# Infini-attention and gated MLP on one core: two head groups share a round of logits, and memory read and update move ahead of the product with V, into its banks

## The chip, the core and the metric

One core of a Trainium2 chip runs the whole program. The metric is device time in microseconds (us). TensorE, VectorE, ScalarE and GpSimd are called PE, DVE, ACT and POOL in the profile; the kernel writes a list of instructions of its own for each (the page of before counts 5369 on PE, 769 on DVE, 347 on ACT and 241 on POOL), and makes them wait for each other through semaphores. All executions quoted are within 1.5% of the fastest of the same kernel; each also reports the mean clock that TensorE was granted, as a share of full speed.

## The reference, cut to what matters

```python
def _A_ref(x, wq, wk, wv, wo, beta):          # H = 32 heads of 32, N = 4 segments of L = 512 tokens
    ...
    for s in range(N):
        qs, ks, vs = ...                      # of this segment
        p = _softmax(einsum('bhqd,bhkd->bhqk', qs, ks) * scale + mask)
        a_dot = einsum('bhqk,bhkd->bhqd', p, vs)
        pq = phi(qs)                          # phi(t) = t + 1 where t > 0, else exp(t)
        num = einsum('bhld,bhde->bhle', pq, M)
        den = einsum('bhld,bhd->bhl', pq, z)[..., None] + 1e-06
        o = g * (num / den) + (1.0 - g) * a_dot
        pk = phi(ks)
        M = M + einsum('bhld,bhle->bhde', pk, vs)
        z = z + einsum('bhld->bhd', pk)
    return o @ wo
h = x + _A_ref(_layernorm(x), ...)            # then h + a gated MLP of _layernorm(h), unchanged here
```

Causal attention inside a segment, plus a read of a memory (M, z) that all earlier segments wrote, mixed by a gate.

## The kernel before

Heads go in groups of four, eight groups a segment, so 32 runs n = 8 s + c of one loop body. Four heads' logits share a round: four matmuls with 32 contraction rows each, one per quarter of the array's rows, into banks 0 to 3; one exponential then evicts all four banks. Because the mask is causal, key chunk j (128 keys) needs 512 - 128 j query columns: rounds of chunk 0 (512 columns), chunks 1 and 3 (384 + 128) and chunk 2 (256). In the unused right half of the third round's banks the memory read is placed.

```python
    def logits(n, rnd):
        parts = {0: ((0, 0, 512),), 1: ((1, 0, 384), (3, 384, 128)), 2: ((2, 0, 256),)}[rnd]
        ...
        for j, o, w in parts:
            for i in range(4):
                pe.matmul(PS[:, i, o:o + w], qk[32 * i:32 * (i + 1), 1, j * 128:(j + 1) * 128],
                          qk[32 * i:32 * (i + 1), 0, j * 128:512], ..., tile_position=(32 * i, 0))
        if rnd == 2 and n >= NQ:
            mem(n)                                   # 4 matmuls into PS[:, cq, 256:388]
        act.activation(e[:, :, 0:wid], PS[:, 0:4, 0:wid], ACTF.Exp, scale=float(SCALE))
        ...                                          # POOL masks the diagonal blocks
        if rnd == 2 and n >= NQ:
            mem_norm(n)                              # DVE: + eps, reciprocal, one 512-wide multiplication

    # a run n (segments 1 and 2)
        logits(n, 0)
        fill(f1)                  # key projection of group n + 1
        pv(n - 1)                 # product with V of the last group: 40 matmuls into banks 4 and 5, then norm on DVE
        logits(n, 1)
        state(n - 1)              # memory update: 4 matmuls into a rotating bank, 2 DVE operations
        bg_pop()                  # a step of a layer norm (DVE)
        fill(f2)                  # query projection of group n + 1
        logits(n, 2)
        phi_exp(n + 1)            # ACT
        fill(f3)                  # half of a V or output projection
        phi_max(n + 1); bg_pop()
        fill(f4); bg_pop()        # the other half
```

Projections use the only two rotating banks, 6 and 7. A recording layer adds a semaphore wait for every hazard; for PSUM it works by whole banks, so that an engine never touches a bank while another one may. That is a choice of the code.

The softmax here doesn't subtract the row's maximum and nothing guards it: scores larger than these inputs give would overflow.

Of the kernel before, what the change touches and what calls it, by code (L numbers as in the profile page):

```python
# [5 lines left out]
BF16 = mybir.dt.bfloat16  # L6
F32 = mybir.dt.float32
I32 = mybir.dt.int32
ACTF = mybir.ActivationFunctionType
# [248 lines left out]
def bass_sequential_preLN__memory_aug_infini_attn__mixer_gmlp__prompt_kernel(  # L258
# [86 lines left out]
    PQK = [b2("pqk%d" % i, [128, 2, L], BF16) for i in range(2)]  # L345
    ETMP = b2("etmp", [128, 2, L], BF16)
    PK = [b2("pk%d" % i, [128, 4, 128], BF16) for i in range(3)]
    E = [[b2("e%d%d" % (k, i), [128, 4, w], BF16) for i, w in enumerate((512, 512, 256))] for k in range(2)]
    TA = b2("ta", [128, 4, 4, 32], F32)
    TM = [b2("tm%d" % i, [128, 4, 4, 32], F32) for i in range(2)]  # L350
    V = b2("v", [128, 4, H, 34], BF16)
# [20 lines left out]
    def bank(b):  # L372
        return PS[:, b, :]

    PVX = PS[:, 4:6, :].rearrange("p b (h w) -> p (b h) w", w=256)
    PVA = PVX[:, :, 0:132].rearrange("p q (i w) -> p q i w", w=33)

    rot = {"banks": list(range(8)), "n": 0}

    def next_bank():  # L380
        b = rot["banks"][rot["n"] % len(rot["banks"])]
        rot["n"] += 1
        return b
# [89 lines left out]
                dve.tensor_copy(d, v)  # L473


    def v_out(s, tcl, half, b):
        o = V[:, tcl, 16 * half:16 * half + 16, 0:32]
        v = bank(b).rearrange("p (h d) -> p h d", d=32)
        if (s, tcl, half) == (0, 3, 0):
            dve.tensor_single_scalar(o, v, RS0[tcl][:], ALU.mult)  # L480
        else:
            act.activation(o, v, ACTF.Copy, scale=RS0[tcl][:] if s == 0 else 1.0)

# [1 line left out]
        pe.matmul(bank(b), XNT[s % 2][:, i, tcl * 128:(tcl + 1) * 128], WV[half][:, i, :],  # L485
                  start=(i == 0), stop=(i == 7))

    def proj_v(s, tcl, half):
        b = next_bank()
        for i in range(8):  # L490
            v_mm(s, tcl, half, b, i)
        v_out(s, tcl, half, b)

    def proj_qk(n, which):
        s, c = divmod(n, NQ)
        b = next_bank()
        xt = XNT[s % 2]
        w = WK if which else WQ
        mm8(bank(b), lambda i: w[:, i, c * 128:(c + 1) * 128], lambda i: xt[:, i, :])
        qk_out(n, which, b)  # L500

    def qk_out(n, which, b):
        if n < NQ:
            dve.tensor_tensor(QK[n % 2][:, which, :], bank(b), RB[:], ALU.mult)
        else:
            act.activation(QK[n % 2][:, which, :], bank(b), ACTF.Copy)

# [16 lines left out]
            sp.dma_start_transpose(PK[n % 3][:], PQK[n % 2][:, 1, :])  # L524


    def logits(n, rnd):
        qk = QK[n % 2]
        parts = {0: ((0, 0, 512),), 1: ((1, 0, 384), (3, 384, 128)), 2: ((2, 0, 256),)}[rnd]
        wid = (512, 512, 256)[rnd]  # L530
        e = E[n % 2][rnd]
        for j, o, w in parts:
            for i in range(4):
                pe.matmul(PS[:, i, o:o + w], qk[32 * i:32 * (i + 1), 1, j * 128:(j + 1) * 128],
                          qk[32 * i:32 * (i + 1), 0, j * 128:512], start=True, stop=True,
                          tile_position=(32 * i, 0))
        if rnd == 2 and n >= NQ:
            mem(n)
        act.activation(e[:, :, 0:wid], PS[:, 0:4, 0:wid], ACTF.Exp, scale=float(SCALE))
        for j, o, w in parts:  # L540
            d = e[:, :, o:o + 128]
            pool.affine_select(out=d, in_=d, pattern=[[0, 4], [1, 128]], compare_op=ALU.is_ge, fill=0.0,
                               base=0, channel_multiplier=-1)
        if rnd == 2 and n >= NQ:
            mem_norm(n)

    def pv(n, cqs=range(4)):
        c = n % NQ
        for cq in cqs:
            for j in range(cq + 1):  # L550
                rnd, o = {0: (0, cq * 128), 1: (1, cq * 128 - 128), 2: (2, cq * 128 - 256), 3: (1, 384)}[j]
                for i in range(4):
                    pe.matmul(PVA[:, cq, i, :], E[n % 2][rnd][:, i, o:o + 128], V[:, j, 4 * c + i, 0:33],
                              start=(cq % 2 == 0 and j == 0 and i == 0), stop=False, skip_group_check=True)
        if 3 in cqs:
            norm(n)

    def mem(n):
        c = n % NQ
        for cq in range(4):  # L560
            pe.matmul(PS[:, cq, 256:388], PQK[n % 2][:, 0, cq * 128:(cq + 1) * 128], MZB[:, c, :, 0:33],
                      start=True, stop=True)

    def mem_norm(n):
        om = PS[:, 0:4, 256:388].rearrange("p q (i d) -> p q i d", d=33)
        dve.tensor_single_scalar(RDM[:], om[:, :, :, 32], float(MEM_EPS), ALU.add)
        dve.reciprocal(RDM[:], RDM[:])
        dve.tensor_tensor(TM[n % 2][:], om[:, :, :, 0:32], RDM[:].unsqueeze(3).to_broadcast([128, 4, 4, 32]), ALU.mult)

    def norm(n):  # L570
        s, c = divmod(n, NQ)
# [9 lines left out]
        if c == NQ - 1:  # L581
            for tcl in range(4):
                to_T(OT, tcl, OTOK[s % 2][:, tcl, :])

    def state(n):
        s, c = divmod(n, NQ)
        if s == NSEG - 1:
            return
        b = next_bank()
        for tcl in range(4):  # L590
            pe.matmul(PS[:, b, 0:132], PK[n % 3][:, tcl, :], V[:, tcl, 4 * c:4 * c + 4, 0:33],
                      start=(tcl == 0), stop=(tcl == 3))
        if s == 0:
            dve.tensor_copy(MSUM[:, c, :], PS[:, b, 0:132])
        else:
            dve.tensor_tensor(MSUM[:, c, :], MSUM[:, c, :], PS[:, b, 0:132], ALU.add)
        dve.tensor_tensor(MZB[:, c, :, 0:33], MSUM[:, c, :].rearrange("p (i d) -> p i d", d=33), MASKG[:, c, :, :],
                          ALU.mult)


    def xr_load(tc):
# [80 lines left out]
    for i in range(4, 8):  # L682
        for t in range(2):
            v_mm(0, t, 0, vb[t], i)
    pe_Th(3, c3, act, dve)
    act_var(3)
    rstd0(3)
    var0(ln_stats(XCH[2]))
    rstd0(2)
    diag(0)  # L690
    v_out(0, 0, 0, vb[0])
    diag(1)
    diag(3)
    diag(2)
    v_out(0, 1, 0, vb[1])
    proj_v(0, 2, 0)
    gates()
# [25 lines left out]
    def z2_group(k, tc, stage=None):  # L723
        s, tcl = divmod(tc, 4)
        b = next_bank()
        wi = WIN[k % 3]
        mm8(PS[:, b, 0:448], lambda i: HNT[s][:, i, tcl * 128:(tcl + 1) * 128], lambda i: wi[:, i, 0:448])
        if stage is None:
            z2_gelu(k, tc, PS[:, b, 0:448])
        else:  # L730
            act.activation(ZSTG[stage][:], PS[:, b, 0:448], ACTF.Copy)
            staged.append((k, tc, ZSTG[stage][:]))

    def z2_gelu(k, tc, src):
# [17 lines left out]
    LAST = NSEG * NQ - 1  # L752
    for n in range(LAST + 1):
        s, c = divmod(n, NQ)
        f1, f2, f3, f4 = [], [], [], []
        if n < LAST:
            f1, f2 = [("qk", n + 1, 1)], [("qk", n + 1, 0)]
        if s == 0:
            f3 = [("v", 0, c, 1)] if c < 4 else [("v", 1, c - 4, 0)]
        elif s < NSEG - 1:  # L760
            if c < 2:
                f3, f4 = [("v", s, 2 * c, 1)], [("v", s, 2 * c + 1, 1)]
            elif c < 6:
                f3, f4 = [("wo", s - 1, c - 2, 0)], [("wo", s - 1, c - 2, 1)]
            else:
                f3, f4 = [("v", s + 1, 2 * (c - 6), 0)], [("v", s + 1, 2 * (c - 6) + 1, 0)]
        elif c < 2:
            f3, f4 = [("v", s, 2 * c, 1)], [("v", s, 2 * c + 1, 1)]
        elif c < 6:
            f3, f4 = [("wo", s - 1, c - 2, 0)], [("wo", s - 1, c - 2, 1)]  # L770
        elif c == 6:
            f3, f4 = [("z2", 0, 4, 0)], [("z2", 0, 5, 1)]
        else:
            f1, f2 = [("z2", 0, 6, 2)], [("z2", 0, 7, 3)]
            f3, f4 = [("z2", 0, 0)], [("z2", 0, 1)]

        def fill(lst):
            for u in lst:
                {"v": proj_v, "wo": wo, "qk": proj_qk, "z2": z2_group}[u[0]](*u[1:])

        if s < NSEG - 1 and c < 4:
            ln_tasks(XCH[c], XNT[(s + 1) % 2], c)
        if s < NSEG - 2 and c >= 4:
            x_load(4 * (s + 2) + c - 4)
        if s > 0 and c == 1:
            xr_load(4 * (s - 1))

        if n == 0:
            fill(f1)
            f1 = [("v", 0, 3, 0)]  # L790
        logits(n, 0)
        fill(f1)
        if n > 0:
            pv(n - 1, range(3) if s == NSEG - 1 else range(4))
        logits(n, 1)
        if s == NSEG - 1:
            pv(n - 1, (3,))
        if n > 0:
            state(n - 1)
        bg_pop()  # L800
        fill(f2)
        logits(n, 2)
        if n < LAST:
            phi_exp(n + 1)
        while n == LAST and staged:
            z2_gelu(*staged.pop(0))
        fill(f3)
        if n < LAST:
            phi_max(n + 1)
        bg_pop()  # L810
        fill(f4)
        bg_pop()
        if n == 1:
            sp.dma_start(WO[:], wcols(A_wo, 0, D))
        if n in (24, 26):
            win_load((n - 24) // 2)
# [101 lines left out]
```

## Time and profile before

| | before |
|---|---|
| time, median (range) | 802.24 us (801.92 to 802.71, 4 runs) |
| granted TensorE clock | 1.000 |
| TensorE busy, by the page | 793.6 us, 99% |
| attention, runs 8 to 31 (first logits to the end of the last product with V, by starts) | 228.1 us |
| two runs of segments 1 and 2 | 19.14 to 19.26 us |

The page's totals and, from its second part, the busy tenths and granted clock in 40 slices:

```profile
PE 793.6 (99%) x5369; PEld 379.8 (47%) x5369; DVE 379.5 (47%) x769; ACT 297.9 (37%) x347; POOL 129.2 (16%) x241
...
PE   8999999999999999999999999999999999999998
...
PEclk9999999999999999999999999999999999999999
```

The ends of matmuls are modelled and overlap (a 512-column matmul of the gated MLP has 379 ns in the page, but 224 of them in a row start 0.216 us apart, 579.04 to 627.39), so 99% busy does not say that nothing is lost. The starts do. This is the timeline of TensorE for one run of segment 2 (start, length, operation, output and inputs, shape, how many; a bracket would be an idle time):

```profile
156.90 0.40 PE L209 MATMUL ps<-qk 32*128 32x512 bf16 x4
157.23 1.90 PE L209 MATMUL ps<-xnT,wk 128*128 128x512 bf16 x8
158.97 1.16 PE L209 MATMUL ps<-v,e 128*128 128x33 bf16 x40
160.05 0.40 PE L209 MATMUL ps<-qk 32*128 32x384 bf16 x8
160.38 0.41 PE L209 MATMUL ps<-v,pk 128*128 128x132 bf16 x4
160.63 1.89 PE L209 MATMUL ps<-xnT,wq 128*128 128x512 bf16 x8
162.45 0.29 PE L209 MATMUL ps<-qk 32*128 32x256 bf16 x4
162.67 0.41 PE L209 MATMUL ps<-mzb,pqk 128*128 128x132 bf16 x4
162.92 3.62 PE L209 MATMUL ps<-wv,xnT 128*128 128x512 bf16 x16
166.47 0.39 PE L209 MATMUL ps<-qk 32*128 32x512 bf16 x4
```

No bracket, no idle time. But the query projection starts at 160.63 and the next round at 162.45: 1.82 us for eight matmuls that owe 8 x 0.216 = 1.73. And that round holds TensorE for 0.22 us (162.45 to 162.67) where its 256 columns owe 0.11 by my estimate (half of the 0.216 for 512 columns, with the four quarters taken as side by side: the four 512-column matmuls of a first round hold TensorE for 0.33 us, 156.90 to 157.23, not for 4 x 0.216). Each round costs about 0.095 us before it and 0.11 after it. That is nearly the whole of what TensorE loses in these runs: from 84 to 310 us, which is all but the start of run 8 and a little after run 31, rounds account for 14.6 of the 15.3 us that starts show beyond the steady spacing of matmuls. Segments 1 to 3 have 72 rounds.

The other engines have their own durations (groups of instructions; busy total, mean ns of one, idle time before them):

```profile
L209 DVE TENSOR_TENSOR tm<-ps,rdm 128x512 f32<-128x512 f32 x24 | 16.6, 692 | 0.8
...
L209 DVE BATCH_NORM_STATS2 stats<-hch 128x6 f32<-128x512 bf16 x32 | 22.1, 690 | 0.6
L209 DVE TENSOR_TENSOR hch<-xr,ps 128x512 bf16<-128x512 bf16 x32 | 21.7, 680 | 5.6 <-PE ps L209 5.1 <-issue 0.5
...
L209 DVE TENSOR_TENSOR msum<-msum,ps 128x132 f32<-128x132 f32 x16 | 4.5, 284 | 0.0
```

And the chain of work that ended last, followed back, is TensorE nearly throughout:

```profile
PE 95%; DVE 4%; ACT 0%; issue 0%
```

### The profile page before, as it was taken

What the parts mean: (1) busy time and instruction counts of PE and PEld (TensorE: products, weight loads), DVE (VectorE), ACT (ScalarE), POOL (GpSimd) and SP (SyncE); (2) the same over time, 40 slices, a digit from 0 to 9 for tenths busy, and PEclk for the clock granted to TensorE, in tenths of its full rate; (3) what the DMA queues carried; (4) which work ended last, traced back from release to release, by engine and by line L of the source; (5) the groups of instructions that cost most, each with busy time, mean ns of one, the idle gap of its engine ahead of it and who ended that gap; (6) DMA issues with size and microseconds to landing.
All of it is one profiled execution on the core that took longest, in us unless ns stands there. A gap on an engine that the chain in (4) does not pass through costs nothing.

```text
span 800.3 us, 12483 instructions
## 1 busy us (share of the span) xinstructions
PE 793.6 (99%) x5369; PEld 379.8 (47%) x5369; DVE 379.5 (47%) x769; ACT 297.9 (37%) x347; POOL 129.2 (16%) x241
## 2 busy tenths in 40 slices
PE   8999999999999999999999999999999999999998
PEld 3444455554454445455544444444444444444444
DVE  6775688579843775844562000053234323323432
ACT  5777877877778675133333333100000000000000
POOL 3543333333333331100131000000000000000000
PEclk9999999999999999999999999999999999999999
DMA  9662535353515324611116000650270143022002
GB/s 295 174 165 53 93 81 120 85 105 84 95 31 127 113 54 112 159 47 53 52 54 132 1 0 1 203 107 7 79 132 1 33 117 69 0 66 47 1 7 86
DMA packets 125000, 64.79 MB, mean 81 GB/s; under 512 B 94992, under 2 KB 113936, under 8 KB 124944
## 3 DMA queue, kind: packets, MB, share of 16 engines
q1 hardware_dynamic: 124944, 63.99, 33.0%
q8 instruction: 42, 0.69, 0.4%
q14 instruction: 14, 0.11, 0.1%
HBM read 32.51 MB, written 8.39 MB: 51 GB/s over the span
## 4 chain that ended last, share of the span: by engine, by line
PE 95%; DVE 4%; ACT 0%; issue 0%
PE ps L209 95%; DVE stats L209 1%; ACT e L209 0%; DVE ta L209 0%; DVE otok L209 0%; DVE hch L209 0%; DVE diag L209 0%; DVE rd L209 0%; DVE xnT L209 0%; DVE pqk L209 0%; DVE lno L209 0%; DVE mv L209 0%; DVE mzb L209 0%; DVE etmp L209 0%; DVE rdm L209 0%
## 5 line engine op out<-in xcount | busy, mean ns | idle before, releaser
L209 PE MATMUL ps<-wspT,z 128*128 128x512 bf16 x896 | 194.0, 379 | 0.0
L209 ACT ACTIVATE e<-ps 128x2048 bf16<-128x2048 f32 (+1 forms) x96 | 152.8, 1592 | 49.3 <-PE ps L209 48.8
L209 PEld LDWEIGHTS ps<-wspT,z 128*128 128x128 bf16 x896 | 87.7, 98 | 105.7
L209 DVE TENSOR_TENSOR tmpg<-ps,brow 128x512 f32<-128x512 f32 x56 | 38.7, 691 | 197.0 <-DMA brow<-in_B_b_sp_dram 105.4
L209 POOL TENSOR_SCALAR_AFFINE_SELECT e<-e 128x512 bf16<-128x512 bf16 x128 | 83.9, 667 | 178.6 <-ACT e L209 178.5
L209 PE MATMUL ps<-win,hnT 128*128 128x448 bf16 x512 | 98.3, 352 | 0.0
L209 PE MATMUL ps<-w_out,yT 128*128 128x512 bf16 (+2 forms) x462 | 97.4, 373 | 0.0
L209 PE MATMUL ps<-hnT,win 128*128 128x512 bf16 x448 | 96.9, 379 | 0.0
L209 PEld LDWEIGHTS ps<-win,hnT 128*128 128x128 bf16 x512 | 49.8, 98 | 46.3 <-issue 0.2
L209 PEld LDWEIGHTS ps<-w_out,yT 128*128 128x128 bf16 x462 | 44.7, 98 | 52.3
L209 PEld LDWEIGHTS ps<-hnT,win 128*128 128x128 bf16 x448 | 43.8, 98 | 52.8
L209 PE MATMUL ps<-xnT,wk 128*128 128x512 bf16 x256 | 60.8, 380 | 0.0
L209 PE MATMUL ps<-xnT,wq 128*128 128x512 bf16 x256 | 60.5, 379 | 0.0
L209 PE MATMUL ps<-wv,xnT 128*128 128x512 bf16 x256 | 59.1, 379 | 0.2 <-ACT xnT L209 0.2
L209 ACT ACTIVATE z<-ps 128x448 bf16<-128x448 f32 x60 | 32.5, 543 | 69.4 <-PE ps L209 69.4
L209 PE MATMUL ps<-wo,oT 128*128 128x512 bf16 x256 | 57.9, 379 | 0.0
L209 ACT ACTIVATE z1T<-ps 128x512 bf16<-128x512 f32 x56 | 33.4, 597 | 63.3 <-PE ps L209 63.3
L209 DVE TENSOR_TENSOR fin<-fin,ps 128x512 bf16<-128x512 bf16 (+2 forms) x33 | 22.1, 671 | 71.3 <-DMA fin<-out_dram 40.8
L209 DVE BATCH_NORM_STATS2 zst<-z 128x6 f32<-128x448 bf16 x64 | 38.9, 620 | 30.1 <-ACT z L209 30.1
L209 PEld LDWEIGHTS ps<-v,e 128*128 128x128 bf16 x1280 | 37.3, 96 | 9.1 <-issue 1.7
L209 DVE TENSOR_TENSOR yT<-tmpg,z1T 128x512 bf16<-128x512 f32 x56 | 38.8, 692 | 1.9
L209 PE MATMUL ps<-v,e 128*128 128x33 bf16 x1280 | 38.4, 177 | 0.0
(83 smaller groups left out, 574.8 us busy)
## 6 DMA issues: line engine op xcount, KB each, us to landing
xch<-in_A_x_dram SPq DMA_DIRECT2D x16, 256.0 KB, 3.0
xr<-in_A_x_dram SPq DMA_DIRECT2D x16, 256.0 KB, 3.2
out_dram<-hch SPq DMA_DIRECT2D x16, 256.0 KB, 2.5
fin<-out_dram SPq DMA_DIRECT2D x16, 256.0 KB, 2.8
out_dram<-fin SPq DMA_DIRECT2D x31, 128.0 KB, 1.7
win<-in_B_w_in_dram SPq DMA_DIRECT2D x4, 896.0 KB, 5.1
w_out<-in_B_w_out_dram SPq DMA_DIRECT2D x1, 3584.0 KB, 13.7
win<-in_B_w_in_dram SPq DMA_DIRECT2D x3, 1024.0 KB, 5.1
```

The lines of the kernel that those rows point to most:

```text
L209: ins = getattr(e, op.name)(*op.args, **op.kw)
```

## The change

The intent: from segment 1 on, the 256-column third rounds of two neighbouring groups fill one 512-column round, so a pair of groups takes five rounds and not six. The memory read can then no longer use the empty half of those banks. It moves, together with the memory update, to a place one run ahead: half of it into bank 5, beside the product with V (which is packed 171 columns apart so that query chunks 0 to 2 stand in bank 4 and chunk 3 in bank 5), the other half into the rotating bank of the update. Some evictions move from ACT to DVE, and the start is reordered a little. The core of the diff (cut: buffers, arguments passed through):

```diff
-    PVX = PS[:, 4:6, :].rearrange("p b (h w) -> p (b h) w", w=256)
-    PVA = PVX[:, :, 0:132].rearrange("p q (i w) -> p q i w", w=33)
+    PSF = PS[:].rearrange("p b n -> p (b n)")
+    PVA = PSF[:, 2048:2048 + 4 * 171].rearrange("p (q w) -> p q w", w=171)[:, :, 0:132]
+    PVA = PVA.rearrange("p q (i w) -> p q i w", w=33)
...
+    def memory(n):
+        s, c = divmod(n, NQ)
+        b = next_bank()
+        if s > 0:
+            mo = [PSF[:, 2700 + 132 * i:2832 + 132 * i] for i in range(2)]        # bank 5
+            mo += [PS[:, b, 132 + 132 * i:264 + 132 * i] for i in range(2)]
+            for cq in range(4):
+                pe.matmul(mo[cq], PQK[n % 2][:, 0, cq * 128:(cq + 1) * 128], MZB[:, c, :, 0:33], ...)
+        if s < NSEG - 1:
+            ...                                             # the update's 4 matmuls into PS[:, b, 0:132]
+        if s > 0:
+            om = [PS[:, b, 132:396], PSF[:, 2700:2964]]
+            ...
+            for k in range(2):                              # + eps; one reciprocal after both
+                dve.tensor_single_scalar(RDM[:, q, :], om[k][:, :, :, 32], float(MEM_EPS), ALU.add)
+            ...
+            for k in range(2):
+                q = slice(2 - 2 * k, 4 - 2 * k)
+                dve.tensor_tensor(TM[n % 2][:, q, :, :], om[k][:, :, :, 0:32], ..., ALU.mult)
+        ...                                                 # msum, mzb on DVE
...
-            f1, f2 = [("qk", n + 1, 1)], [("qk", n + 1, 0)]
+            f1 = [("qk", n + 1, 1, act if first else dve)]  # first: n is even
+            f2 = [("qk", n + 1, 0)]
...
+        if s > 0 and not first:
+            logits([(n - 1, 2), (n, 2)])                    # the shared round
+            fill(f1)
+            memory(n - 1)
+            bg_pop()
+            logits([(n, 0)])
+            fill(f2)
+            pv(n - 1)
+            logits([(n, 1), (n, 3)])
+            if n == LAST:
+                memory(n)
+        elif s > 0:
+            logits([(n, 0)])
+            fill(f1)
+            memory(n - 1)
+            pv(n - 1)
+            bg_pop()
+            logits([(n, 1), (n, 3)])
+            fill(f2)
```

and in the start:

```diff
+    var0(ln_stats(XCH[2]))
+    rstd0(2)
     pe_Th(3, c3, act, dve)
     act_var(3)
     rstd0(3)
-    var0(ln_stats(XCH[2]))
-    rstd0(2)
     ...
+    diag(2)
     diag(3)
-    diag(2)
```

More of the change, by code (lines that the diff above doesn't have):

```diff
@@ L347, in bass_sequential_preLN__memory_aug_infini_attn__mixer_gmlp__prompt_kernel @@
     PK = [b2("pk%d" % i, [128, 4, 128], BF16) for i in range(3)]
-    E = [[b2("e%d%d" % (k, i), [128, 4, w], BF16) for i, w in enumerate((512, 512, 256))] for k in range(2)]
+    E = [[b2("e%d%d" % (k, i), [128, 4, 512], BF16) for i in range(2)] for k in range(2)]
+    E2 = b2("e2", [128, 4, 512], BF16)
     TA = b2("ta", [128, 4, 4, 32], F32)
@@ L473, in pe_T, with v_out @@
                 dve.tensor_copy(d, v)
-    def v_out(s, tcl, half, b):
+    def v_out(s, tcl, half, b, eng=act):
         o = V[:, tcl, 16 * half:16 * half + 16, 0:32]
@@ L480, in v_out @@
             dve.tensor_single_scalar(o, v, RS0[tcl][:], ALU.mult)
+        elif eng is dve:
+            dve.tensor_copy(o, v)
         else:
@@ L486, in v_mm, with proj_v @@
                   start=(i == 0), stop=(i == 7))
-    def proj_v(s, tcl, half):
+    def proj_v(s, tcl, half, eng=act):
         b = next_bank()
@@ L491, in proj_v, with proj_qk @@
             v_mm(s, tcl, half, b, i)
-        v_out(s, tcl, half, b)
-    def proj_qk(n, which):
+        v_out(s, tcl, half, b, eng)
+    def proj_qk(n, which, eng=act):
         s, c = divmod(n, NQ)
@@ L499, in proj_qk, with qk_out @@
         mm8(bank(b), lambda i: w[:, i, c * 128:(c + 1) * 128], lambda i: xt[:, i, :])
-        qk_out(n, which, b)
-    def qk_out(n, which, b):
+        qk_out(n, which, b, eng)
+    def qk_out(n, which, b, eng=act):
         if n < NQ:
             dve.tensor_tensor(QK[n % 2][:, which, :], bank(b), RB[:], ALU.mult)
+        elif eng is dve:
+            dve.tensor_copy(QK[n % 2][:, which, :], bank(b))
         else:
@@ L524, in phi_max, with e_of, logits @@
             sp.dma_start_transpose(PK[n % 3][:], PQK[n % 2][:, 1, :])
-    def logits(n, rnd):
-        qk = QK[n % 2]
-        parts = {0: ((0, 0, 512),), 1: ((1, 0, 384), (3, 384, 128)), 2: ((2, 0, 256),)}[rnd]
-        wid = (512, 512, 256)[rnd]
-        e = E[n % 2][rnd]
-        for j, o, w in parts:
+    def e_of(n, j, cq):
+        o = (cq - j) * 128
+        if j == 2:
+            return E2, 256 * (n % 2) + o
+        return E[n % 2][j % 2], o + (384 if j == 3 else 0)
+    def logits(parts):
+        for n, j in parts:
+            qk = QK[n % 2]
+            e, o = e_of(n, j, j)
+            w = 512 - 128 * j
             for i in range(4):
@@ L536, in logits @@
                           tile_position=(32 * i, 0))
-        if rnd == 2 and n >= NQ:
-            mem(n)
-        act.activation(e[:, :, 0:wid], PS[:, 0:4, 0:wid], ACTF.Exp, scale=float(SCALE))
-        for j, o, w in parts:
+        lo = e_of(*parts[0], parts[0][1])[1]
+        hi = o + w
+        act.activation(e[:, :, lo:hi], PS[:, 0:4, lo:hi], ACTF.Exp, scale=float(SCALE))
+        for n, j in parts:
+            o = e_of(n, j, j)[1]
             d = e[:, :, o:o + 128]
@@ L543, in logits @@
                                base=0, channel_multiplier=-1)
-        if rnd == 2 and n >= NQ:
-            mem_norm(n)
     def pv(n, cqs=range(4)):
@@ L550, in pv @@
             for j in range(cq + 1):
-                rnd, o = {0: (0, cq * 128), 1: (1, cq * 128 - 128), 2: (2, cq * 128 - 256), 3: (1, 384)}[j]
+                e, o = e_of(n, j, cq)
                 for i in range(4):
-                    pe.matmul(PVA[:, cq, i, :], E[n % 2][rnd][:, i, o:o + 128], V[:, j, 4 * c + i, 0:33],
-                              start=(cq % 2 == 0 and j == 0 and i == 0), stop=False, skip_group_check=True)
+                    pe.matmul(PVA[:, cq, i, :], e[:, i, o:o + 128], V[:, j, 4 * c + i, 0:33],
+                              start=(cq % 3 == 0 and j == 0 and i == 0), stop=False, skip_group_check=True)
@@ L555, in pv @@
         if 3 in cqs:
             norm(n)
-    def mem(n):
-        c = n % NQ
-        for cq in range(4):
-            pe.matmul(PS[:, cq, 256:388], PQK[n % 2][:, 0, cq * 128:(cq + 1) * 128], MZB[:, c, :, 0:33],
-                      start=True, stop=True)
-    def mem_norm(n):
-        om = PS[:, 0:4, 256:388].rearrange("p q (i d) -> p q i d", d=33)
-        dve.tensor_single_scalar(RDM[:], om[:, :, :, 32], float(MEM_EPS), ALU.add)
-        dve.reciprocal(RDM[:], RDM[:])
-        dve.tensor_tensor(TM[n % 2][:], om[:, :, :, 0:32], RDM[:].unsqueeze(3).to_broadcast([128, 4, 4, 32]), ALU.mult)
+    def memory(n):
[5 more added lines that the diff above has]
+            for cq in range(4):
+                pe.matmul(mo[cq], PQK[n % 2][:, 0, cq * 128:(cq + 1) * 128], MZB[:, c, :, 0:33],
+                          start=True, stop=True)
+        if s < NSEG - 1:
+            for tcl in range(4):
+                pe.matmul(PS[:, b, 0:132], PK[n % 3][:, tcl, :], V[:, tcl, 4 * c:4 * c + 4, 0:33],
+                          start=(tcl == 0), stop=(tcl == 3))
+        if s > 0:
+            om = [PS[:, b, 132:396], PSF[:, 2700:2964]]
+            om = [m.rearrange("p (q i d) -> p q i d", q=2, d=33) for m in om]
+            for k in range(2):
+                q = slice(2 - 2 * k, 4 - 2 * k)
+                dve.tensor_single_scalar(RDM[:, q, :], om[k][:, :, :, 32], float(MEM_EPS), ALU.add)
+                if k == 1:
+                    dve.reciprocal(RDM[:], RDM[:])
+            for k in range(2):
+                q = slice(2 - 2 * k, 4 - 2 * k)
+                dve.tensor_tensor(TM[n % 2][:, q, :, :], om[k][:, :, :, 0:32],
+                                  RDM[:, q, :].unsqueeze(3).to_broadcast([128, 2, 4, 32]), ALU.mult)
+        if s == 0:
+            dve.tensor_copy(MSUM[:, c, :], PS[:, b, 0:132])
+        elif s < NSEG - 1:
+            dve.tensor_tensor(MSUM[:, c, :], MSUM[:, c, :], PS[:, b, 0:132], ALU.add)
+        if s < NSEG - 1:
+            dve.tensor_tensor(MZB[:, c, :, 0:33], MSUM[:, c, :].rearrange("p (i d) -> p i d", d=33),
+                              MASKG[:, c, :, :], ALU.mult)
@@ L583, in norm @@
                 to_T(OT, tcl, OTOK[s % 2][:, tcl, :])
-    def state(n):
-        s, c = divmod(n, NQ)
-        if s == NSEG - 1:
-            return
-        b = next_bank()
-        for tcl in range(4):
-            pe.matmul(PS[:, b, 0:132], PK[n % 3][:, tcl, :], V[:, tcl, 4 * c:4 * c + 4, 0:33],
-                      start=(tcl == 0), stop=(tcl == 3))
-        if s == 0:
-            dve.tensor_copy(MSUM[:, c, :], PS[:, b, 0:132])
-        else:
-            dve.tensor_tensor(MSUM[:, c, :], MSUM[:, c, :], PS[:, b, 0:132], ALU.add)
-        dve.tensor_tensor(MZB[:, c, :, 0:33], MSUM[:, c, :].rearrange("p (i d) -> p i d", d=33), MASKG[:, c, :, :],
-                          ALU.mult)
     def xr_load(tc):
@@ L730, in z2_group @@
         else:
-            act.activation(ZSTG[stage][:], PS[:, b, 0:448], ACTF.Copy)
+            if stage == 1:
+                dve.tensor_copy(ZSTG[stage][:], PS[:, b, 0:448])
+            else:
+                act.activation(ZSTG[stage][:], PS[:, b, 0:448], ACTF.Copy)
             staged.append((k, tc, ZSTG[stage][:]))
@@ L754, in bass_sequential_preLN__memory_aug_infini_attn__mixer_gmlp__prompt_kernel @@
         s, c = divmod(n, NQ)
+        first = n % 2 == 0
         f1, f2, f3, f4 = [], [], [], []
         if n < LAST:
-            f1, f2 = [("qk", n + 1, 1)], [("qk", n + 1, 0)]
+            f1 = [("qk", n + 1, 1, act if first else dve)]
+            f2 = [("qk", n + 1, 0)]
+        last = dve if first else act
         if s == 0:
             f3 = [("v", 0, c, 1)] if c < 4 else [("v", 1, c - 4, 0)]
-        elif s < NSEG - 1:
-            if c < 2:
-                f3, f4 = [("v", s, 2 * c, 1)], [("v", s, 2 * c + 1, 1)]
-            elif c < 6:
-                f3, f4 = [("wo", s - 1, c - 2, 0)], [("wo", s - 1, c - 2, 1)]
-            else:
-                f3, f4 = [("v", s + 1, 2 * (c - 6), 0)], [("v", s + 1, 2 * (c - 6) + 1, 0)]
         elif c < 2:
-            f3, f4 = [("v", s, 2 * c, 1)], [("v", s, 2 * c + 1, 1)]
+            f3, f4 = [("v", s, 2 * c, 1)], [("v", s, 2 * c + 1, 1, last)]
         elif c < 6:
             f3, f4 = [("wo", s - 1, c - 2, 0)], [("wo", s - 1, c - 2, 1)]
+        elif s < NSEG - 1:
+            f3, f4 = [("v", s + 1, 2 * (c - 6), 0)], [("v", s + 1, 2 * (c - 6) + 1, 0, last)]
         elif c == 6:
@@ L790, in bass_sequential_preLN__memory_aug_infini_attn__mixer_gmlp__prompt_kernel @@
             f1 = [("v", 0, 3, 0)]
-        logits(n, 0)
-        fill(f1)
-        if n > 0:
-            pv(n - 1, range(3) if s == NSEG - 1 else range(4))
-        logits(n, 1)
-        if s == NSEG - 1:
-            pv(n - 1, (3,))
-        if n > 0:
-            state(n - 1)
-        bg_pop()
-        fill(f2)
-        logits(n, 2)
+        if n == NQ:
+            rot["n"] = 0
+        if s > 0 and not first:
[17 more added lines that the diff above has]
+            fill(f2)
+        else:
+            logits([(n, 0)])
+            fill(f1)
+            if n > 0:
+                pv(n - 1)
+            logits([(n, 1), (n, 3)])
+            if n > 0:
+                memory(n - 1)
+            bg_pop()
+            fill(f2)
+            logits([(n, 2)])
         if n < LAST:
```

## The prediction

> **What bounds it.** TensorE. The page shows it 99% busy, but its matmul ends are modelled, so I looked at starts. In the timeline, 128x512 matmuls start every 0.216 us and a head group of segments 1 and 2 takes 9.57 us (9.33 in segment 3). It owes 32 of them (6.91), the product with V (40 x 25 ns), memory read and state (8 x 59 ns) and logits worth 0.55: 8.9. The missing 0.6 are three rounds of logits: about 0.095 us before each and 0.11 after it. No other wait shows. [...]
>
> **Removed.** Segments 1 to 3 have 72 rounds, then 60. 12 x 0.205 = 2.5 us, all on the critical path. The saved exponential overhead (2 x 1.02 against 1.88 us) and the evictions moved to VectorE free ScalarE, which TensorE does not wait for. In the start, the first key projection waits 0.58 us and the next matmul 0.18 for the diagonal tiles; the reordering should give 0.6 us back.
>
> **Added: two new waits of TensorE on VectorE.**
>
> 1. In even runs (n = 10, 12, ... 30: 11 of them) the memory read of group n-1 stands directly before the product with V of the same group. Half the read lies in bank 5, where the product's last query chunk goes, so its 16 matmuls must wait until VectorE has read the memory: the built order shows a new wait there. [...] Only 24 x 25 ns = 0.6 us of product covers it. VectorE needs about 0.17 to start, 0.6 for sums and reciprocal, and two 256-wide multiplications at about 0.42 (from 0.28 for 132 and 0.69 for 512): 1.6 us. Stall about 0.95 us when VectorE is free. It isn't after runs with an output projection: eviction (0.68), layer-norm statistics (1.42+0.21) and phi stand before. In the trace those end 3 to 4 us after a run's first logits; the memory read is there at 2.5. I estimate 2.0 us (n = 12, 20), 1.5 (14, 22), 1.3 (28, 30) and 0.95 for the other five: about 14 us.
>
> 2. In odd runs VectorE evicts the next keys (about 0.65 us), behind those statistics, and only two banks rotate, so the query projection needs that bank 2.9 us into the run. Runs 11, 13, 19, 21, 27 and 29 should lose 0.5 to 0.9 each: about 4 us; less if VectorE catches up during the first stall.
>
> Sum: 14 to 18 us, less 3.
>
> **Predicted:** 816 us, 8 in 10 between 808 and 823. Faster by over 2%: 0.02; within 2%: 0.68; slower by over 2%: 0.30.
>
> **In the profile:** 12 rounds fewer; each still costs 0.2 us beyond its columns. The product's last 16 matmuls in even runs from n = 10 start late by 0.9 us or more; odd runs after output projections stop before the query projection, waiting for VectorE's key copy. Odd runs otherwise 9.67 us, even ones 9.36 plus the stall. Exponentials of logits: 60 in segments 1 to 3, not 72. All after the attention unchanged (0.216 per matmul).
>
> **What would make it wrong:** if the wait at the last chunk is met early, 799.5 us. If VectorE's backlog is shorter, 809. If VectorE saturates, or ScalarE's evictions fall behind the merged exponential, above 823.

802.2 + 16 (the middle of 14 to 18) - 3 is about 815, put at 816. The 0.17 us for VectorE's start and the 0.42 for a 256-wide multiplication are estimates. In the trace of before VectorE starts on the last product with V 0.19 us after the next matmul does (308.25 to 308.44), and in the changed kernel two such multiplications took 0.76 us.

## The result

| | before | changed |
|---|---|---|
| time, median (range, 4 runs each) | 802.24 us (801.92 to 802.71) | 822.53 us (821.82 to 824.52) |
| ratio | 1 | 1.0256 (95%: 1.0236 to 1.0276) |
| granted clock of the four runs | 1.000 (profiled run) | 0.994, 0.998, 0.998, 0.996 |
| pair of runs 10+11, 12+13, 14+15 (profiled execution) | 19.26, 19.26, 19.14 us | 20.65, 23.38, 22.31 us |

A ratio is the mean time of one kernel's runs over that of the other's of the same rounds, so it is not quite the ratio of the medians. The changed kernel is slower by 2.6%. The time of a pair is read from the start of an even run's first logits to that of the next even run. The changed kernel's profiled execution is the slowest of its four; the pairs 12+13 and 14+15 contain stretches at half clock, shown below.

The page and the chain of the changed kernel:

```profile
PE 797.9 (97%) x5369; PEld 382.6 (46%) x5369; DVE 400.6 (49%) x835; ACT 288.2 (35%) x317; POOL 130.2 (16%) x241
...
PE 86%; DVE 10%; DMA 2%; issue 1%; ACT 0%; DVEq 0%
```

VectorE has got onto the chain. Who made TensorE wait (the view of waits: total us, times, longest):

```profile
PE ps L209 <- DVE tm L209: 13.6, 11, 2.1
PE ps L209 <- DVE qk L209: 3.5, 7, 0.7
...
PE ps L209 <- DVE ta L209: 1.0, 1, 1.0
...
PE ps L209 <- DMA pk<-pqk: 0.5, 1, 0.5
```

Before, the largest entry of this list was 1.7 us at the very start. The first line is the memory term (tile tm), 11 times; the second the copy of the next keys (tile qk). Here is the longest of the 11, in run 12, on all engines (POOL and weight loads cut):

```profile
120.80 0.68 DVE L209 TENSOR_TENSOR hch<-xr,ps 128x512 bf16<-128x512 bf16 x1
...
121.32 0.51 PE L209 MATMUL ps<-mzb,pqk 128*128 128x132 bf16 x4
...
121.85 1.42 DVE L209 BATCH_NORM_STATS2 stats<-hch 128x6 f32<-128x512 bf16 x2
121.90 0.76 PE L209 MATMUL ps<-v,e 128*128 128x33 bf16 x24
123.30 0.21 DVE L209 BATCH_NORM_AGGREGATE mv<-stats 128x2 f32<-128x12 f32 x1
123.43 0.18 DVE L209 TENSOR_SCALAR rdm<-ps 128x8 f32<-128x8 f32 x2
...
123.93 0.76 DVE L209 TENSOR_TENSOR tm<-ps,rdm 128x256 f32<-128x256 f32 x2
...
124.74 0.64 PE L209 MATMUL ps<-v,e 128*128 128x33 bf16 x16 [2.09 <-DVE tm L209]
...
125.86 2.96 PE L209 MATMUL ps<-xnT,wq 128*128 128x512 bf16 x8
```

The first 24 matmuls of the product are done at about 122.5. VectorE is still at layer-norm statistics of the run before; it reads the memory from 123.43 to 124.69, and only then may the last 16 matmuls write bank 5. They use nothing that VectorE computes there; they share a bank with the memory read, not data (by the diff, the product's chunk 3 has columns 1 to 132 of bank 5 and the memory read columns 140 to 403).

The last line shows something that nobody asked for. Eight matmuls of the query projection took 2.79 us from start to start of what follows, not 1.73. The view of windows has the granted clock (PE's busy time first; PEclk is 1.00 at full speed), in stretches of 3.41 us:

```profile
121.20:124.62 3.42, 1.46 (x34) 1.12 (x32) 3.28 (x11) 0.91 (x2) 1.57 (x3) 1.00 0.72 159
124.62:128.03 3.41, 3.29 (x30) 1.45 (x31) 2.38 (x7) 1.88 (x1) 0.10 (x1) 0.50 1.02 254
```

In the stretch from 121.20 TensorE worked 1.46 of 3.42 us; in the next one its granted clock was 0.50. This happened three times in the profiled run (from 124.62, 148.51 and 233.85), each time for 3.41 us, and these starts lie 7 and 25 times 3.413 us apart. The stretches of 3.41 us just before held 1.46, 1.93 and 1.94 us of work: they have the waits of runs 12, 14 and 22 (2.3, 1.65 and 1.65 us by starts). Not every such wait was followed by half clock. That of run 20 was 2.3 us too, and 208.24 to 211.65 held 1.32 us of work, but the clock stayed at 1.00; counted in the same steps of 3.413 us it falls across two stretches (206.53 to 209.94 and 209.94 to 213.36, with 2.41 and 2.33 us of work). What decides it the trace does not show, and I draw no threshold from it. In the unprofiled runs the mean clock was 0.998, 0.998 and 0.996, by my estimate one, one and two halved stretches (each is 3.41 x 0.5 / 822 = 0.2%), and the times go with it: 821.99 and 821.82, then 823.07, and 824.52 in the profiled run with three (0.994).

The second kind of wait, in run 11 (an odd one): the statistics of the run before end at 111.7, the keys' copy follows, and the query projection waits for its bank:

```profile
110.27 1.41 DVE L209 BATCH_NORM_STATS2 stats<-hch 128x6 f32<-128x512 bf16 x2
...
111.84 0.64 DVE L209 CAST qk<-ps 128x512 bf16<-128x512 f32 x1
...
112.54 1.90 PE L209 MATMUL ps<-xnT,wq 128*128 128x512 bf16 x8 [0.67 <-DVE qk L209]
```

Added up from starts in the two profiled runs (each sum is what TensorE spends between starts beyond steady spacing and beyond the usual 0.09 to 0.11 us of a round):

| TensorE time, changed minus before | us |
|---|---|
| 11 waits before the product's last chunk (0.98 five times; 2.3, 1.65 and 1.35 twice each) | +15.5 |
| waits before the query projection in odd runs (0.74 four times, 0.29 to 0.44 three times, small rest) | +4.2 |
| three stretches at half clock | +4.6 |
| last run: its memory read waits for the product's last reader in bank 5 (1.0), and its first round for the exponential of the shared round (0.2) | +1.2 |
| run 1: the update waits for the DMA of the transposed keys | +0.5 |
| 12 rounds fewer | -2.5 |
| start: no wait for diagonal tiles | -0.8 |
| four small waits of before that are gone | -0.5 |
| sum | +22.2 |

The spans differ by 822.8 - 800.3 = 22.5 us. Everything after the attention has the same matmul spacing (0.216 us at 512 columns) in both.

### The profile page after: what moved, and what is told of

It reads as the page before. It is cut to its first block, busy times and chain, and to the rows that moved or that the text cites. A ratio compares the mean times of both kernels' runs of the same rounds, so it can differ in the third digit from the quotient of the medians.

```text
span 822.8 us, 12515 instructions
## 1 busy us (share of the span) xinstructions
PE 797.9 (97%) x5369; PEld 382.6 (46%) x5369; DVE 400.6 (49%) x835; ACT 288.2 (35%) x317; POOL 130.2 (16%) x241
## 4 chain that ended last, share of the span: by engine, by line
PE 86%; DVE 10%; DMA 2%; issue 1%; ACT 0%; DVEq 0%
PE ps L209 86%; DVE stats L209 3%; DVE hch L209 2%; DMA pk<-pqk 1%; DVE tm L209 1%; DVE lno L209 1%; DVE rdm L209 1%; DVE pqk L209 1%; DVE etmp L209 1%; DVE qk L209 0%; DVE mv L209 0%; DMA xch<-in_A_x_dram 0%; DVE ta L209 0%; ACT e L209 0%; DVE mzb L209 0%
## 5 line engine op out<-in xcount | busy, mean ns | idle before, releaser
L209 ACT ACTIVATE e<-ps 128x2048 bf16<-128x2048 f32 (+1 forms) x84 | 150.8, 1795 | 88.0 <-PE ps L209 88.0
L209 POOL TENSOR_SCALAR_AFFINE_SELECT e<-e 128x512 bf16<-128x512 bf16 x128 | 80.6, 646 | 197.3 <-ACT e L209 197.1
L209 PE MATMUL ps<-xnT,wq 128*128 128x512 bf16 x256 | 64.3, 397 | 3.5 <-DVE qk L209 3.5
L209 DVE TENSOR_TENSOR fin<-fin,ps 128x512 bf16<-128x512 bf16 (+2 forms) x33 | 22.2, 671 | 71.3 <-DMA fin<-out_dram 39.3
L209 DVE BATCH_NORM_STATS2 zst<-z 128x6 f32<-128x448 bf16 x64 | 38.9, 620 | 30.1 <-ACT z L209 30.1
L209 PE MATMUL ps<-v,e 128*128 128x33 bf16 x1280 | 38.9, 178 | 13.6 <-DVE tm L209 13.6
```

The costliest lines, as they stand in the source:

```text
L209: ins = getattr(e, op.name)(*op.args, **op.kw)
```

## The experiments

Theory A: VectorE's reading of bank 5 holds up the product (and its late copy of the keys the next projection); the idle TensorE then loses its clock. Rival B: VectorE is simply overloaded by the work moved to it (its busy time rose from 379.5 to 400.6 us), and the waits would turn up wherever it is needed next. Rival C: the shared round with its wide exponential holds up ScalarE. All kernels gave correct results. Times are medians; "before" ran beside each.

| run | us (range) | ratio to before (95%) |
|---|---|---|
| changed | 822.53 (821.82 to 824.52) | 1.0256 (1.0236 to 1.0276) |
| e1_split | 805.57 (805.23 to 805.96) | 1.0040 (1.0025 to 1.0055) |
| e2_keyact | 817.29 (815.42 to 818.54) | 1.0184 (1.0168 to 1.0199) |
| e3_both, and again | 802.09 (801.88 to 802.51), 802.18 (802.05 to 802.47) | 0.9997 (0.9982 to 1.0012), 0.9996 (0.9982 to 1.0010) |
| e4_busy | 819.48 (819.39 to 819.76) | 1.0214 (1.0197 to 1.0231) |
| e5_bank5first | 817.13 (816.38 to 819.35) | 1.0181 (1.0165 to 1.0197) |
| e6_start | 801.59 (801.45 to 801.88) | 0.9991 (0.9979 to 1.0004) |
| e7_best | 823.20 (822.87 to 823.34) | 1.0257 (1.0243 to 1.0271) |
| e8_rounds | 804.41 (804.04 to 804.60) | 1.0023 (1.0010 to 1.0035) |
| e9_best | 800.41 (799.80 to 800.72) | 0.9973 (0.9960 to 0.9987) |

### e1_split: the last chunk later

```diff
             memory(n - 1)
-            pv(n - 1)
+            pv(n - 1, range(3))
             bg_pop()
             logits([(n, 1), (n, 3)])
             fill(f2)
+            pv(n - 1, (3,))
```

> Changed kernel, but in even runs of segments 1 to 3 the product's last query chunk (the 16 matmuls that write bank 5) comes after the query projection instead of straight after the memory read. Theory A (TensorE waits because bank 5 is still being read): the 11 waits, 15.5 us in the trace of the changed kernel, vanish, and with them the half-clock stretches (5 us there); waits for the key copy may grow a little. 803 to 807 us, granted clock 1.000. Rival B (VectorE has simply too much work since evictions were moved to it, and the wait would turn up wherever VectorE is needed next): above 815 us, the wait now before the product's first chunk of odd runs or at a projection. Rival C (the merged third round holds up ScalarE): unchanged, 822.

Measured: 805.57 us, clock 1.000 in all four runs. TensorE in run 12, and its waits:

```profile
121.48 0.76 PE L209 MATMUL ps<-v,e 128*128 128x33 bf16 x24
122.17 0.40 PE L209 MATMUL ps<-qk 32*128 32x384 bf16 x8
122.50 1.90 PE L209 MATMUL ps<-xnT,wq 128*128 128x512 bf16 x8
124.23 0.56 PE L209 MATMUL ps<-v,e 128*128 128x33 bf16 x16
```

```profile
PE ps L209 <- DVE qk L209: 5.0, 7, 1.3
```

The first kind of wait is gone from the list, no stretch has half clock any more, and 17 of the 20 us are back, although VectorE does exactly the same work. B and C fall as main causes. What is left is mostly the second kind: it grew from 4.2 to 5.7 us, most likely because VectorE no longer gets time to catch up from the first.

### e2_keyact: the next keys evicted by ScalarE again

```diff
-            f1 = [("qk", n + 1, 1, act if first else dve)]
+            f1 = [("qk", n + 1, 1)]
```

> Changed kernel with the keys always evicted by ScalarE, as before the change. Theory A: only the waits of odd runs before the query projection go (4.0 us beyond the usual 0.11 after a round), so about 818 us; waits in even runs stay at 15 us. Rival B (VectorE overloaded): 12 x 0.65 = 8 us of work leave VectorE, and the even runs' waits shrink as well: 812 us or less. Rival C: ScalarE gets more work, slower than 822.

Measured: 817.29 us. The odd runs' waits fall from 4.2 to 0.6 us (three of 0.19 remain in segment 3, where ScalarE's copy stands behind its exponential). The 11 waits of even runs hardly change, from 15.5 to 15.2 us by starts, although about 8 us of work left VectorE (its busy time fell from 400.6 to 391.5 us). In the view of waits, where the changed kernel has 13.6:

```profile
PE ps L209 <- DVE tm L209: 13.4, 11, 2.0
```

So not the amount of VectorE's work sets them, but what stands in its queue at that moment. The four runs also order themselves by clock: 815.42 us at 1.000, 817.21 and 817.37 at 0.998, 818.54 at 0.996.

### e3_both

The two edits above together.

> Both edits. Theory A: all but the rounds and small waits gone: 802.2 - 2.5 for the 12 rounds and + 1.4 for the wait of the last run's memory read = about 801 us, 799 to 803. Rival B: over 810. Rival C: 822.

Measured: 802.09 us, and 802.18 in a second set; the two edits together remove the changed kernel's loss (ratio to before 0.9997). It is not faster than before, though it has 12 rounds fewer. Its waits name most of what ate the 2.5 us:

```profile
PE ps L209 <- DVE ta L209: 1.0, 1, 1.0
PE ps L209 <- DVE hch L209: 0.9, 2, 0.4
PE ps L209 <- DMA pk<-pqk: 0.4, 1, 0.4
```

The last run's memory read; two waits of runs 12 and 20 for a bank that VectorE evicts late (by starts these two runs take 12.72 and 12.71 us where their neighbours take 11.88); the start's DMA.

### e4_busy: idle time filled, waits left alone

```diff
             memory(n - 1)
-            pv(n - 1)
+            pv(n - 1, range(3))
+            busy({12: 84, 20: 84, 14: 56, 22: 56, 28: 44, 30: 44}.get(n, 28 if n > NQ else 0))
+            pv(n - 1, (3,))
```

`busy(k)` issues k matmuls of 38 columns into columns of bank 4 that nobody reads; the 84 of run 12 took 2.25 us from start to start, 27 ns each.

> Changed kernel, with 28 to 84 idle-filling matmuls (38 columns, 25 ns each, into an unused corner of bank 4, never read) put into each of the 11 waits, sized a little under the wait. Theory A says the wait itself is set by VectorE and stays; if the half-clock stretches come from TensorE's idle time they vanish: granted clock 1.000 in every run and about 819.5 us, 818.5 to 820.5, with runs agreeing within 0.5 us (the changed kernel's spread over 2.7). If the stretches do not come from idle time: 822 to 824 with clock 0.994 to 0.998 as before.

Measured: 819.48 us, four runs within 0.4, clock 1.000 in all. The same place as above, run 12, in its timeline, and the same two stretches in windows:

```profile
121.53 0.76 PE L209 MATMUL ps<-v,e 128*128 128x33 bf16 x24
122.13 2.25 PE L209 MATMUL ps<-ident 128*128 128x38 bf16 x84
124.38 0.57 PE L209 MATMUL ps<-v,e 128*128 128x33 bf16 x16
```

```profile
121.20:124.62 3.42, 3.42 (x125) 3.33 (x125) 3.25 (x11) 0.55 (x2) 1.56 (x3) 1.00 0.82 190
124.62:128.03 3.41, 3.41 (x35) 1.62 (x32) 2.04 (x5) 2.68 (x3) 0.76 (x2) 1.00 1.17 163
```

Work of no use makes the kernel 3 us faster (the medians, 822.53 to 819.48) and steadier. The wait itself stays: run 12 takes 14.23 us, against 15.58 in the changed kernel, which lost about 1.3 there to the half clock. The half clock is a second cost of the idle time, on top of the wait; it is also the source of the changed kernel's spread (2.7 us at mean clocks of 0.994 to 0.998, against 0.4 us here at 1.000). Not all of the 3 us need be clock: the changed kernel's own four executions, with one, one, two (by their mean clocks) and three halved stretches, lie 1.2 to 1.5 us a stretch apart.

### e5_bank5first: the same reads in another order

```diff
-            for k in range(2):
+            for k in (1, 0):
                 q = slice(2 - 2 * k, 4 - 2 * k)
                 dve.tensor_tensor(TM[n % 2][:, q, :, :], om[k][:, :, :, 0:32],
```

> Changed kernel with the order of VectorE's two multiplications of the memory read turned round, so that bank 5 is read for the last time one multiplication (about 0.34 us start to start) earlier; VectorE does the same work. Theory A: each of the 11 waits shrinks by 0.34 us, 3.7 us in sum, and there may be one half-clock stretch fewer: about 818 us, 817 to 819.5. Rival B (load of VectorE): no change, 822.5.

Measured: 817.13 us. In the trace each of the 11 waits is 0.33 us shorter (by starts, sum 11.9 for 15.5; 81 of the 5369 matmul records are missing from this trace, none inside these waits). The view of waits, against 13.6 before the edit:

```profile
PE ps L209 <- DVE tm L209: 10.0, 11, 1.8
```

Two of the four runs had clock 1.000 and took 816.38 and 816.74. Against e4_busy, also at full clock, that is 2.9 us; 3.6 were to be expected. The two ran on different chips, and the filler's own cost is in e4_busy, so I do not read more into the difference. So the end of the wait moves with the last read of bank 5, not with the end of the memory read. No run puts the two uses into different banks; that it is the shared bank rests on this run, on e1_split and on the columns in the code.

### e6_start: the start order alone, on the kernel before

The edit is the second diff of the change, and nothing else of it.

> The kernel before with nothing but the changed start order (third chunk's statistics first, diagonal tiles in order). In the traces the changed start reaches its first logits at 19.28 us instead of 20.06, but loses 0.54 again in the second run, where the state's matmuls wait for the transposed keys' DMA. If that DMA's landing is set by the loads queued before it, this kernel gains at most 0.3 us over before: 802.0. If the 0.54 is due to something else in the changed kernel, it gains 0.7 to 0.8: 801.5.

Measured: 801.59 us, 0.7 less than before by the medians, but the interval (0.9979 to 1.0004) contains no change. In its trace the two waits for the diagonal tiles (0.58 and 0.18 us) are gone, but the mean granted clock of this execution was 0.999, where before had 1.000; 0.1% of 800 us is 0.8 us, by this estimate as much as the two waits, so the trace does not tell whether the update in run 1 would wait. In the changed kernel, e1_split and e3_both, which reach that update earlier, its matmuls start at about 30.1 us; in before it arrives at 30.36 and does not wait. But the DMA did not land at one time: in the traces its first transfer landed at 30.07 us in the changed kernel, 30.06 in e3_both and 29.66 in the second execution of that same kernel, 30.52 in e9_best, 29.62 in before and 28.54 in this run. So whether run 1 waits differs from execution to execution. The time is nearer to the second forecast (801.5), but what the start gives stays open between 0 and 0.7 us.

### e8_rounds: the price of a round by itself

e3_both with 12 more rounds, one in each even run of segments 1 to 3 between `f3` and `f4`:

```diff
+        if s > 0 and first:
+            for i in range(4):
+                pe.matmul(PS[:, i, 0:128], QK[n % 2][32 * i:32 * (i + 1), 1, 0:128],
+                          QK[n % 2][32 * i:32 * (i + 1), 0, 0:128], ..., tile_position=(32 * i, 0))
         fill(f4)
```

> e3_both with 12 extra rounds of logits (four 32-row matmuls of 128 columns, results overwritten before anyone reads them), one in each even run of segments 1 to 3 between two projections. If a round costs 0.205 us beyond its columns, as read from the trace of before, each adds 0.205 + 0.056 = 0.26 us: e3_both + 3.1 = 805.2 us, 804.6 to 805.8. If a round costs only its columns and the 0.2 us is an artefact of the profile, e3_both + 0.7 = 802.8.

Measured: 804.41 us, 2.2 more than e3_both beside it, just under the range. The trace shows both halves of the price at every added round (0.10 us before, 0.11 after, beyond 0.056 for the columns: 12 x 0.26 = 3.2), here in run 10:

```profile
104.59 1.89 PE L209 MATMUL ps<-wo,oT 128*128 128x512 bf16 x8
106.41 0.23 PE L209 MATMUL ps<-qk 32*128 32x128 bf16 x4
106.58 1.90 PE L209 MATMUL ps<-wo,oT 128*128 128x512 bf16 x8
```

In the same trace the waits of runs 12 and 20 shrink by 1.1 us in sum (from 0.61 to 0.19 before the last half of the memory read, from 0.21 to 0.09 before the last chunk, in each of the two), most likely because the added rounds give VectorE time to catch up; that makes the difference. The columns alone would have added 0.7 us, so the price of a round is real time and no artefact of the profile; by the trace, 12 rounds are worth 2.5 us to a TensorE that waits for nothing else. What in a round costs this is not shown apart.

### e7_best and e9_best: is there a version that beats both?

e7_best put three moves on e3_both: the last chunk's layer-norm statistics for the next segment from run c = 3 to c = 6, the matmuls of one MLP group ahead of the last memory read, and the first update behind the V projection of run 1. Its edits for the first and third:

```diff
-        if s < NSEG - 1 and c < 4:
-            ln_tasks(XCH[c], XNT[(s + 1) % 2], c)
+        if s < NSEG - 1 and c in ((0, 1, 2, 3) if s == 0 else (0, 1, 2, 6)):
+            ln_tasks(XCH[min(c, 3)], XNT[(s + 1) % 2], min(c, 3))
...
-            if n > 0:
+            if n > 1:
                 memory(n - 1)
...
         fill(f3)
+        if n == 1:
+            memory(0)
```

The second is in e9_best's diff below, without its line that changes `rot`.

> e3_both and three moves off waits that its trace still shows: the last chunk's statistics of the next segment from run c=3 to c=6 (2 x 0.8 us of waits in runs 12 and 20), the last memory read behind one z2 group (1.2 us), the first state behind the V projection of run 1 (0.45 us wait for a DMA). Theory A (these are the remaining waits, TensorE is otherwise full): 802.1 - 3.3 = 798.8 us, 798 to 800, faster than before by 0.4%. If those waits only hide others that come next: 801 to 802.

Measured: 823.20 us, a plain miss of mine, with clocks of 0.988 to 0.990. Its waits say why:

```profile
PE ps L209 <- DMA xnT<-lno: 12.5, 2, 6.2
PE ps L209 <- ACT z L209: 3.8, 1, 3.8
```

The key projection of a next segment's first group already stands in run c = 7, so the chunk came 6.2 us too late, twice; and with only two rotating banks the group I moved blocked the next one until a gelu had run, which ScalarE does after everything else. The part aimed at did work: runs 12 and 20 went from 12.71 to 11.88 us. e9_best mends both (also on e3_both; cut: the two lines that set `rot` after the loop are gone):

```diff
-        if s < NSEG - 1 and c < 4:
+        if s < NSEG - 1 and c < (4 if s == 0 else 3):
             ln_tasks(XCH[c], XNT[(s + 1) % 2], c)
+        if 0 < s < NSEG - 1 and c == 0:
+            ln_tasks(XCH[3], XNT[(s + 1) % 2], 3)
...
             if n == LAST:
+                f3, bl = [], next_bank()
+                mm8(PS[:, bl, 0:448], lambda i: HNT[0][:, i, 0:128], lambda i: WIN[0][:, i, 0:448])
                 memory(n)
+                rot["banks"], rot["n"] = [0, 1, 2, 3, 6, 7, 4, 5], 0
...
+        if n == LAST:
+            z2_gelu(0, 0, PS[:, bl, 0:448])
         fill(f3)
```

> e7's two mistakes mended: the last chunk's statistics now come in run c=0 (e7 had them so late that the next segment's first key projection waited 6.2 us for the transposed chunk, twice), the group after the last memory read takes a free logits bank (e7: 3.8 us wait for a gelu), and the first state stays where it was. Runs 12 and 20 should keep e7's 11.88 us (12.71 in e3_both), the last run lose 1 us: 802.2 - 2.7 = 799.5 us, 798.8 to 800.5. If the work moved to run c=0 makes VectorE late there, 801 to 802.

Measured: 800.41 us, ratio 0.9973 (0.9960 to 0.9987): 0.3% faster than before, in an interval that excludes no change. Pairs of runs of segments 1 and 2 take 18.92 us, all but the first (18.68) and 16+17 (19.41), where before took 19.14 to 19.26, which is one round less (and the small waits). Its trace has one wait of 0.5 us in run 16, from the statistics moved there, some of 0.2 to 0.3 in the last segment, and this remains of the start:

```profile
PE ps L209 <- DMA pk<-pqk: 1.0, 1, 1.0
```

## Why the prediction was right, and what it missed

The prediction (816 us, 808 to 823) held with 822.5, but only 0.5 us below its upper end, and one of the four executions (824.52) lies above it. It favoured "within 2%" with 0.68; "slower by over 2%", which came, had 0.30. The mechanism was right and its sizes were close; that the range still held 822.5, with the clock and the last run missing from the sum, is in part luck. Point by point:

- **What bounds the kernel: right.** TensorE with 0.2 us lost per round. The trace of the changed kernel has 60 rounds in segments 1 to 3 at the same price, and e8_rounds measured it by itself.
- **The wait for bank 5: right, in place and number, and nearly in size.** 11 waits were forecast at about 14 us in sum; they measured 15.5 (0.95 forecast for a free VectorE, 0.98 measured; 2.0, 1.5 and 1.3 forecast behind statistics, 2.3, 1.65 and 1.35 measured). e1_split removed them, e5_bank5first shortened them by moving one read.
- **The wait for the copied keys: right.** About 4 us forecast, 4.2 measured. The runs were not quite the six named: run 25 lost 0.29 us too, and runs 27 and 29 only 0.29 and 0.44.
- **Missed: the clock.** "Sum: 14 to 18 us, less 3" counted waiting time only. The granted clock also fell to 0.50 for three stretches in the profiled execution, 4.6 us (mean clock 0.994; 0.996 to 0.998 in the other three), and for none in e4_busy, where the idle time is filled (1.000 in all four): up to 3 us between the medians of the two.
- **Missed: the last run.** Its memory read stands behind the product's last reader in bank 5: 1.0 us, the same hazard the other way round (1.2 with the wait for the exponential before it).
- **Half wrong: the start.** "the reordering should give 0.6 us back": the waits went (0.76 us), but 0.54 came back in run 1 of the profiled execution behind a DMA. e6_start does not settle what it is worth alone.
- The alternatives named as dangers did not come: ScalarE's evictions did not fall behind to any cost beyond that 0.2 us, and VectorE's load as such did not set the waits (e1_split, e2_keyact).

The mid-sum of the forecast was 16 - 3 = 13 us; the measured waits (19.7), the last run, the rounds and the start together give about 17 to 18 us; the clock adds the rest.

## What to carry to other kernels

When two uses share a PSUM bank and the kernel guards by whole banks, as here, the second waits for the last reader of the first, whatever columns they use: ask how much independent work of the writing engine stands between them, and compare it with the reader's time plus everything queued in front of the reader. Placing 16 matmuls 2.2 us later was worth 17 us here, while the saving that the change was made for was 2.5. And idle time of TensorE was paid for twice here: after three of its four waits of 1.65 to 2.3 us the granted clock was 0.50 for 3.41 us, 4.6 us in all in the profiled execution. Look at the granted clock of every run: here the means went from 0.994 to 0.998 over four executions of the same kernel, and the times from 824.52 to 821.82.
